# Summing spectral products by 32x32 blocks of the identity in place of 64x64 blocks

## The chip, the core and the metric

The kernel runs on one core of one Trainium2 chip. The metric is the device time of one execution in microseconds (us); lower is better. The core has a matrix engine (TensorE, PE in the profile; its weight loads are listed apart as PEld), a vector engine (VectorE, DVE), an activation engine (ScalarE, ACT), GpSimd (POOL) and SyncE (SP), which here only issues DMAs. Matmuls write to PSUM, 8 banks of 512 fp32 values on each of 128 partitions; ACT and DVE copy from there to SBUF.

## The reference, cut to what matters

The output is two results side by side, for 2048 positions and 576 channels each. A is a dilated sliding-window attention (32 heads of 18, window 8, step 2) with its projections; it is not touched by the change. B is a long convolution, which the reference computes by FFT:

```python
kv = k_shift * v                                   # [1, 2048, 576], k_shift: a 4-tap filter of k
kv_f = rfft(pad(kv, S)); kf_f = rfft(pad(ssm_k, S))  # along the positions, length 4096
y_f = kv_f * kf_f
y = irfft(y_f)[:S].astype(bfloat16) + kv * ssm_D
b = q * y
```

## The kernel before, in words

**Part B by blocks.** The positions are cut into four blocks of 512 (`NBL`, `BL`). For each input block i, matmuls with sine and cosine tables give its spectrum, 512 frequencies by 576 channels as a cosine part and a sine part (`x_spectrum`, L579). The filter's four blocks get their spectra in the same way (`filter_spectrum`, L520, kept in `Ks`). Output block j is the inverse transform of a sum over i = 0..j of complex products, spectrum of block i times filter spectrum of block j - i.

**Frequencies and partitions.** A spectrum has 128 partitions and four groups of frequencies (g) beside each other. For the inverse transform, each 64-row half of the partitions takes part of its groups from the other half, so the sums also move rows from one half to the other.

**Products, sums, inverse.** The work list `todo` (L979) has 30 entries (j, t, i): for each output block j, three thirds t of the channels (192 each, `TH`), and for each of those the blocks i = 0..j. For each entry:

- `products` (L856) is one DVE instruction (L860), 3072 elements per partition: both parts of the input's spectrum times both parts of the filter's. Its result goes to one of four places in `qk`, in turn (L858). Products run two entries ahead of the sums (`LEAD`, L983).
- `sums` (L867) adds the products into PSUM on PE (L880), as matmuls with blocks of the identity or of its negative (`ident`, `identn`) as weights. The real half is cosine by cosine and sine by sine, the imaginary half sine by cosine and cosine by sine. Each half (r) has a tile `acc[r]` of two banks, taken at i = 0. One call has 16 matmuls of 64x64 blocks with 384 columns, 4 for each of the 4 terms: `s` goes over two pairs of frequency groups, `h` over the two halves of the partitions.
- At i = j the two tiles are copied to `Yall` (L893 on ACT; the very last one by DVE, L891).
- When all channels of a block are there, `inverse` (L900) does matmuls with the table `TI` (L912), copies (L915), matmuls that mirror rows (`back`, L953), copies (L960), and a gate on DVE that multiplies with q (`gate`, L966), ahead of the store. For the last block the last third goes through `last` (L925, matmuls L931, copies L933, `ps_back` L939) and `gate_last` (L921).

`TI` is made early, from the table `TX`, by `table_i` (L384): identity matmuls (L390) that transpose and rearrange, 16 per call in two calls, then two copies each on ACT (L394).

**What sets the order.** Each engine runs its instructions in the order in which the program issues them. The script writes them in an order that it plans itself: `units` is a queue of PE work (output projection `ps_wo` L792 and L784, inverse steps), from which `until()` takes as many at each step as the table `PLACES` says; `tasks` is a queue of DVE work with due times (`due`), which a simple clock `clk` for D (DVE), P (PE) and A (ACT) estimates. `sums` calls `until()` first, and adds 0.34 us per half to the P clock. PSUM is given out under two tags of two buffers each, one buffer being two banks (`bank2`): tag A for the projections and the inverse, tag B for the sums, the attention sums (`ps_acc`, copied by L743 and L757) and others. A buffer is given out again when its copy is done. DVE, ACT, SP and POOL are in-order queues as well, so an instruction that waits holds up those behind it.

Of the kernel before, what the change touches and what calls it, by code (L numbers as in the profile page):

```python
# [24 lines left out]
def view(t, offset, dims):  # L25

    return bass.AP(tensor=t.tensor, offset=t.offset + offset, ap=[list(t.ap[0])] + [list(d) for d in dims])
# [3 lines left out]
def kernel(  # L31
# [13 lines left out]
    nc = tc.nc  # L45
    Bsz, S, D = A_x.shape
# [22 lines left out]
    NBL, BL = 4, 512  # L69
# [5 lines left out]
    TH = 192  # L75
# [12 lines left out]
    def bank2(name, tag):  # L88
        return pp.tile([128, 2, 512], FP32, name=name, tag=tag)
# [9 lines left out]
    TX = main.tile([128, 4, BL], BF16, name="TX", tag="tabx")  # L99
    TI = main.tile([128, 4, 2, 256], BF16, name="TI")  # L100
# [115 lines left out]
    ident = main.tile([128, 128], BF16, name="ident")  # L216
# [18 lines left out]
    for c0, p0, p1 in ((0, 0, 128), (128, 0, 128), (256, 0, 128), (384, 0, 128), (512, 0, 64), (512, 64, 128)):  # L235
        EHS.append(main.tile([128, 32], BF16, name=f"E{len(EHS)}"))
        e = EHS[-1][p0:p1, :]
# [20 lines left out]
    clk = {"D": 0.0, "P": 0.0, "A": 0.0}  # L258
    psum = {"A": deque([0.0, 0.0]), "B": deque([0.0, 0.0])}
# [7 lines left out]
    def pe(us, tag, evac, ready=0.0, first=True, last=True):  # L267

        clk["P"] = max(clk["P"], ready, psum[tag].popleft() if first else 0.0) + us
        clk["A"] = max(clk["A"], clk["P"] + 0.1) + evac  # L270
        if last:
            psum[tag].append(clk["A"])
        return clk["A"]
# [8 lines left out]
    def until():  # L282

        for _ in range(next(places, 0)):
            if units:
                p = max(clk["P"], psum["A"][0] if psum["A"] else 0.0)
                pop(next((n for n, u in enumerate(units) if len(u) < 4 or u[3] <= p), 0))
# [93 lines left out]
        return table(n_all[:, 2 * n:2 * n + 2, :], TX[:, 2 * n:2 * n + 2, :], n_all[:, 8, :], (4 + 2 * n, 5 + 2 * n), 4096,  # L381
              (offx[:], offx[:]))

    def table_i(s):  # L384

        ps = bank2("ps_ti", "A")
        for g2 in range(2):
            for c in range(4):
                for o in range(2):
                    nc.tensor.matmul(ps[64 * o:64 * o + 64, g2, 128 * c:128 * c + 128],  # L390
                                     view(TX, c * BL + 128 * (2 * ((o - s) % 2) + g2) + 64 * s, [[1, 64]]),
                                     ident[:], start=True, stop=True, tile_position=(0, 64 * o))
        for g2 in range(2):
            nc.scalar.activation(view(TI, 1024 * s + 512 * g2, [[128, 4], [4, 32], [1, 4]]),  # L394
                                 view(ps, 512 * g2, [[32, 4], [1, 32], [128, 4]]), ACT.Copy)

    skb = sp1.tile([128, 4, D], BF16, name="skb")
# [35 lines left out]
    for n0 in range(0, D, 256):  # L433
        n = min(256, D - n0)
        ps = bank2("ps_sk", "A" if n == 256 else "B")
        for h in range(0, n, 128):
            w = min(128, n - h)
            sk = skrow[:, 4 * (n0 + h):4 * (n0 + h + w)].rearrange("p (d j) -> p d j", j=4)
            for r in range(2):
                nc.tensor.matmul(ps[64 * r:64 * r + 64, h // 128, 0:4 * w], onesb[:, 0:64],  # L440
                                 sk if r else view(skrow, 4 * (n0 + h) + 3, [[4, w], [-1, 4]]),
                                 start=True, stop=True, tile_position=(0, 64 * r))
# [29 lines left out]
    for n in range(2):  # L472
        units.insert(2 + 4 * n, (0.85, partial(early, partial(table_i, n), 0.85), "x"))
# [5 lines left out]
    def taps(i):  # L479
        kj, vt = kjs[i], vts[i]  # L480
        kv = ab[:, i].rearrange("p s c d -> p (s c) d")
        for j in (3, 2, 1, 0):
            o = kv if j == 3 else sp1.tile([128, 4, D], BF16, name="tB")[:]
            dve(2304, lambda: nc.vector.tensor_tensor(  # L484
                o, kj[:, 3 - j:7 - j, :], skb[:, 3 - j, :].unsqueeze(1).to_broadcast([128, 4, D]), ALU.mult))
            if j < 3:
                dve(2304, lambda: nc.vector.tensor_tensor(kv, kv, o, ALU.add))  # L487
        return dve(2304, lambda: nc.vector.tensor_tensor(kv, kv, vt[:], ALU.mult))
# [57 lines left out]
    for i in range(NBL):  # L546
        r = taps(i)
# [51 lines left out]
    for jj, i in ((0, 0), (1, 2)):  # L599
# [6 lines left out]
        for n in range(2):  # L606
            a, b = last[4 * n:4 * n + 4], rest[4 * n:4 * n + 4]
# [221 lines left out]
    Yall = main.tile([128, 2, 2, 4, D], BF16, name="Yall", tag="r_kv")  # L829
# [35 lines left out]
    acc = {}  # L865

    def sums(j, t, i, pr, ready):  # L867

        until()
        sc, ss = CSG[j - i], SSG[j - i]  # L870
        for r, terms in enumerate((((0, 0, sc), (1, 1, ss)), ((1, 0, sc), (0, 1, -ss)))):
            if i == 0:
                acc[r] = bank2("ps_z", "B")
                clk["P"] = max(clk["P"], psum["B"][r])
            for n, (part, cs, sign) in enumerate(terms):
                w = ident if sign > 0 else identn
                for s in range(2):
                    for h in range(2):
                        o = 64 * ((h + s) % 2)
                        nc.tensor.matmul(view(acc[r], 512 * h, [[192, 2], [96, 2], [1, 96]])[o:o + 64], w[64 * h:64 * h + 64, 64 * h:64 * h + 64],  # L880
                                         pr[64 * h:64 * h + 64, part, cs, :].rearrange(
                                             "p (a g e) -> p g a e", a=2, g=4)[:, 2 * s:2 * s + 2],
                                         start=(i == 0 and n == 0), stop=(i == j and n == 1),
                                         tile_position=(64 * h, o))
            clk["P"] = max(clk["P"], ready) + 0.34
        if i == j:
            for r in range(2):
                y, z = (view(Yall, (j % 2) * 8 * D + r * 4 * D + TH * t, [[2 * D, 2], [D, 2], [1, TH]]),
                        view(acc[r], 0, [[512, 2], [TH, 2], [1, TH]]))
                if (j, t, r) == (NBL - 1, 2, 1):  # L890
                    nc.vector.tensor_copy(y, z)  # L891
                else:
                    nc.scalar.activation(y, z, ACT.Copy)  # L893
                out = pe(0.0, "B", 0.85)
            return out
# [102 lines left out]
    for n, (j, t, i) in enumerate(todo):  # L998
        produce(n + LEAD)
        if (t, i) == (0, 0):  # L1000
            need(f"inv{j - 2}")
        r = sums(j, t, i, *prs.pop(n))
        new = []
        if i == j and t == 2 and j < NBL - 1:
            a, b = inverse(j, 0, HD, r), inverse(j, HD, HD, r)
            new = [a[0], b[0], a[1], b[1], a[2], b[2]]
        elif i == j and j == NBL - 1 and t > 0:
            new = inverse(j, 0, 2 * TH, r) if t == 1 else inverse(j, 2 * TH, TH, r)
        for u in new:
            units.insert(sum(w[2][:3] == "inv" for w in units), u)  # L1010
# [35 lines left out]
```

## Time and profile before

| | us |
|---|---|
| median of 3 runs (224.27 to 224.85) | 224.3 |
| the profiled execution | 225.0 |
| its span, first to last instruction | 223.0 |
| PE busy / DVE busy / ACT busy in the span | 213.1 / 208.1 / 154.4 |
| L860 products on DVE, 30 of 1.75 | 50.5 |
| L893 copies of the sums on ACT, 23 of 0.81 | 17.4 |

The profile is one execution, traced by the hardware. An engine's row says how long at least one of its instructions was running. Matmuls overlap each other, so a busy PE may still take more work; 64x64 matmuls in different quarters of the array run at the same time. A group of instructions is written as line, engine, operation, output<-inputs, shapes, count, then busy time and mean duration (ns) of one, then the engine's idle time before them and what ended it. The timeline has start, length, engine and instruction, with idle time before it in brackets. The chain of waits goes back from the last instruction to what released it; it runs on PE for most of the first 194 us and mostly on DVE from then on. The stage with the products and sums is 160 to 216 us.

### The profile page before, as it was taken

To read this page: it belongs to the slowest core of one execution; us is meant where nothing else is said; L and a number is where in the kernel's file an instruction comes from. 1 tells how busy PE (TensorE), PEld (TensorE's weight loads), DVE (VectorE), ACT (ScalarE), POOL (GpSimd) and SP (SyncE) were. 2 spreads that over 40 slices of the span, in tenths; PEclk is the share of its full clock that TensorE was granted. 3 is DMA by queue.
4 is the path that set the end of the run, shared out by engine and by line. 5 is a ranking of instruction groups with operands and counts; after the bars stand their busy time and mean duration, and the time that the engine had idled before them with its cause. 6 is when DMAs were issued, how large, how long until landed. Compare 5 with 4: busy or idle time off the path is not lost.

```text
span 223.0 us, 5309 instructions
## 1 busy us (share of the span) xinstructions
PE 213.1 (96%) x2271; PEld 118.2 (53%) x2271; DVE 208.1 (93%) x156; ACT 154.4 (69%) x213; POOL 31.9 (14%) x68
## 2 busy tenths in 40 slices
PE   7999999999999999999999999999999999999891
PEld 2543444444566556753444445665656667666560
DVE  7789999999988999999899999999999899999992
ACT  5858766888596987756667768885678887655630
POOL 8860000000000040403410000015000000330000
PEclk9999999999999999999999999999999999999999
DMA  5999999999900047659999469917211103662016
GB/s 187 274 229 219 188 241 203 221 207 235 216 0 0 3 83 131 117 95 169 198 190 235 124 114 203 225 32 234 88 56 53 57 3 107 199 208 75 3 53 159
DMA packets 30985, 31.41 MB, mean 141 GB/s; under 512 B 16849, under 2 KB 26705, under 8 KB 30962
## 3 DMA queue, kind: packets, MB, share of 16 engines
q1 hardware_dynamic: 25714, 21.93, 44.6%
q0 software_dynamic: 2624, 6.64, 14.6%
q10 hardware_dynamic: 2624, 2.51, 3.3%
q8 instruction: 17, 0.28, 0.5%
q14 instruction: 6, 0.05, 0.1%
HBM read 13.11 MB, written 4.72 MB: 80 GB/s over the span
## 4 chain that ended last, share of the span: by engine, by line
PE 76%; DVE 9%; ACT 5%; issue 4%; DMA 3%; SPq 1%; DVEq 0%; ACTq 0%
PE ps_proj L310 15%; PE ps_fk L515 10%; PE ps_wo L792 7%; PE ps_fx L586 6%; DVE qk L860 6%; PE ps_z L880 5%; PE ps_log L633 5%; PE ps_fk L516 5%; PE ps_acc L739 4%; PE ps_inv L912 4%; PE ps_proj L427 3%; PE ps_proj L315 3%; DMA X<-attn 3%; PE ps_proj L322 3%; PE ps_idle L138 2%
## 5 line engine op out<-in xcount | busy, mean ns | idle before, releaser
L860 DVE TENSOR_TENSOR qk<-xw,Ks 128x3072 bf16<-128x3072 bf16 x30 | 50.5, 1750 | 1.2 <-PE ps_z L880 1.0
L624 DVE TENSOR_TENSOR prod<-qk 128x4096 bf16<-128x4096 bf16 (+1 forms) x20 | 40.6, 2074 | 3.4 <-PE ps_log L633 3.3
L310 PE MATMUL ps_proj<-xw 128*128 128x512 bf16 x160 | 38.4, 380 | 0.0
L515 PE MATMUL ps_fk<-kTok,TK 128*128 128x384 bf16 x128 | 32.8, 327 | 0.6 <-ACT Ks L530 0.5
L516 PE MATMUL ps_fk<-kTok,TK 128*128 128x192 bf16 x128 | 31.4, 246 | 0.0
L530 ACT ACTIVATE Ks<-ps_fk 128x576 bf16<-128x576 f32 x32 | 20.4, 653 | 9.9 <-PE ps_fk L516 9.7
L310 PEld LDWEIGHTS <-xw 128*128 128x128 bf16 x160 | 14.3, 98 | 18.9 <-issue 4.9
L893 ACT ACTIVATE Yall<-ps_z 128x768 bf16<-128x768 f32 x23 | 17.4, 808 | 6.1 <-PE ps_z L880 5.9
L346 ACT ACTIVATE qk<-ps_proj 128x1024 bf16<-128x1024 f32 x14 | 14.4, 1027 | 7.1 <-PE ps_proj L310 3.4
L589 ACT ACTIVATE xw<-ps_fx 128x576 bf16<-128x576 f32 x32 | 18.6, 660 | 0.2
L515 PEld LDWEIGHTS <-TK 128*128 128x128 bf16 x128 | 12.5, 98 | 11.8 <-issue 4.2
L792 PE MATMUL ps_wo<-qk,pv 128*128 128x288 bf16 x128 | 17.9, 287 | 0.0
L586 PE MATMUL ps_fx<-ab,TX 64*128 64x288 bf16 x256 | 17.7, 283 | 0.0
L487 DVE TENSOR_TENSOR ab<-ab,tB 128x2304 bf16<-128x2304 bf16 x12 | 16.3, 1358 | 0.4
L880 PE MATMUL ps_z<-qk,ident 64*64 64x384 bf16 x288 | 16.4, 325 | 0.3 <-ACT pv L743 0.3
L484 DVE TENSOR_TENSOR tB<-kj,skb 128x2304 bf16<-128x2304 bf16 x12 | 16.3, 1356 | 0.3
L912 PE MATMUL ps_inv<-Yall,TI 128*128 128x288 bf16 (+1 forms) x112 | 15.5, 292 | 0.7 <-ACT Yall L893 0.6
L739 PE MATMUL ps_acc<-P,ident 64*64 64x512 bf16 x192 | 15.3, 379 | 0.0
L346 ACT ACTIVATE v<-ps_proj 128x1024 bf16<-128x1024 f32 x9 | 9.2, 1022 | 8.8 <-PE ps_proj L322 4.6
L586 PEld LDWEIGHTS <-TX 64*128 64x128 bf16 x256 | 11.7, 94 | 6.5 <-issue 3.6
L799 ACT ACTIVATE qk<-ps_wo 128x576 bf16<-128x576 f32 x16 | 10.4, 651 | 6.1 <-PE ps_wo L792 3.0
L792 PEld LDWEIGHTS <-pv 128*128 128x128 bf16 x128 | 11.5, 98 | 6.0 <-issue 3.2
(146 smaller groups left out, 352.8 us busy)
## 6 DMA issues: line engine op xcount, KB each, us to landing
kj<-in_B_k_dram SPq DMA_DIRECT2D x7, 504.0 KB, 8.1
Ks<-Ks POOLq DMA_DIRECT2D x6, 576.0 KB, 7.7
qk<-attn SPq DMA_DIRECT2D x12, 256.0 KB, 5.8
vt<-in_B_v_dram SPq DMA_DIRECT2D x8, 288.0 KB, 8.6
out_dram<-qk ACTq DMA_DIRECT2D x8, 288.0 KB, 2.9
X<-attn SPq DMA_DIRECT2D x8, 256.0 KB, 5.1
Ks<-in_A_x_dram SPq DMA_DIRECT2D x2, 576.0 KB, 5.2
xw<-in_A_wqkv_dram SPq DMA_DIRECT2D x2, 576.0 KB, 7.4
```

Source lines behind the costliest of these rows:

```text
L310: nc.tensor.matmul(ps[:, jp, :], wq(kb, comp, 128 * ct, 128), xT(kb, 1024 * jj + 512 * jp, 512), start=(kb == 0 and not first), stop=(kb = ...
L346: nc.scalar.activation(view(t, o + pad + 1024 * jj, [[512, 2], [1, 512]]), ps[:], ACT.Copy)
L515: nc.tensor.matmul(o[:, 0:2], w, rhs[:, 0:2], start=start, stop=stop)
L516: nc.tensor.matmul(o[:, 2], w, rhs[:, 2], start=start, stop=stop)
L530: nc.scalar.activation(view(Ks, (3 - m) * SPB + 4 * D * cs + 96 * gi, [[768, 3], [384, 2], [1, 96]]), acc3(ps), ACT.Copy, scale=(CSG, SSG) ...
L586: nc.tensor.matmul(ps[:, pm, 0:HD], TX[64 * pm:64 * pm + 64, c, 128 * gi:128 * gi + 128], kv[64 * pm:64 * pm + 64, c, HD * h:HD * h + HD], ...
L624: r = dve(1024 * nj, lambda: nc.vector.tensor_tensor(view(prod, 0, [[256 * nj, 4], [256, nj], [1, 256]]), view(t, o + 256 * hh, [[0, 4], [ ...
L739: nc.tensor.matmul(acc[64 * o:64 * o + 64, h, :], ident[64 * h:64 * h + 64, 64 * h:64 * h + 64], view(P, 256 * u, [[2048, 2], [1, 256]])[6 ...
L792: nc.tensor.matmul(ps[:, r, 0:HD], oT(hh, j + 2 * r, t)[:, o:o + 128], wo[:, t // 2, t % 2, HD * h:HD * h + HD], start=(t == 0 and h == 0) ...
L860: r = dve(3072, lambda: nc.vector.tensor_tensor(pr, view(xw, i * SPB + 4 * TH * t, [[4 * D, 2], [0, 2], [1, 4 * TH]]), view(Ks, (3 - j + i ...
L880: nc.tensor.matmul(view(acc[r], 512 * h, [[192, 2], [96, 2], [1, 96]])[o:o + 64], w[64 * h:64 * h + 64, 64 * h:64 * h + 64], pr[64 * h:64 ...
L912: nc.tensor.matmul(ps[:, c, 0:n], TI[:, sl, pm, 128 * c:128 * c + 128], Yall[:, j % 2, pm, sl, c0:c0 + n], start=(pm == 0 and sl == 0), st ...
```

## The change

In `sums`, the identity blocks have 32 rows and 32 columns in place of 64, and a matmul has 192 columns in place of 384. One call has 64 matmuls and as many weight loads, in place of 16. The rows of each of the four 32-row groups (s) go to a PSUM bank of their own: groups 0 and 1 to the two banks of `acc[0]`, 2 and 3 to those of `acc[1]`. The real half takes the first 192 columns of a bank, the imaginary half the next 192, so each bank holds both. Both tiles are taken at the start of an i = 0 call. The frequencies that end up in one row group of `Yall` are other ones than before, so `table_i` arranges `TI` to fit: 32 matmuls of 32 columns per call in place of 16 of 64. The copies to `Yall` now take one pair of row groups each, both halves of it. The script's P clock gets 0.2 per half in place of 0.34. Nothing else changes.

```diff
-    def table_i(s):
+    def table_i(n):
...
         for g2 in range(2):
+            s = 2 * n + g2
             for c in range(4):
-                for o in range(2):
-                    nc.tensor.matmul(ps[64 * o:64 * o + 64, g2, 128 * c:128 * c + 128],
-                                     view(TX, c * BL + 128 * (2 * ((o - s) % 2) + g2) + 64 * s, [[1, 64]]),
-                                     ident[:], start=True, stop=True, tile_position=(0, 64 * o))
+                for o in range(4):
+                    nc.tensor.matmul(ps[32 * o:32 * o + 32, g2, 128 * c:128 * c + 128],
+                                     view(TX, c * BL + 128 * ((o - s) % 4) + 32 * s, [[1, 32]]),
+                                     ident[:], start=True, stop=True, tile_position=(0, 32 * o))
...
         sc, ss = CSG[j - i], SSG[j - i]
+        if i == 0:
+            for n in range(2):
+                acc[n] = bank2("ps_z", "B")
+                clk["P"] = max(clk["P"], psum["B"][n])
         for r, terms in enumerate((((0, 0, sc), (1, 1, ss)), ((1, 0, sc), (0, 1, -ss)))):
-            if i == 0:
-                acc[r] = bank2("ps_z", "B")
-                clk["P"] = max(clk["P"], psum["B"][r])
             for n, (part, cs, sign) in enumerate(terms):
                 w = ident if sign > 0 else identn
-                for s in range(2):
-                    for h in range(2):
-                        o = 64 * ((h + s) % 2)
-                        nc.tensor.matmul(view(acc[r], 512 * h, [[192, 2], [96, 2], [1, 96]])[o:o + 64], w[64 * h:64 * h + 64, 64 * h:64 * h + 64],
-                                         pr[64 * h:64 * h + 64, part, cs, :].rearrange(
-                                             "p (a g e) -> p g a e", a=2, g=4)[:, 2 * s:2 * s + 2],
-                                         start=(i == 0 and n == 0), stop=(i == j and n == 1),
-                                         tile_position=(64 * h, o))
-            clk["P"] = max(clk["P"], ready) + 0.34
+                for g in range(4):
+                    for s in range(4):
+                        o = 32 * ((s + g) % 4)
+                        nc.tensor.matmul(view(acc[s // 2], 512 * (s % 2) + TH * r, [[96, 2], [1, 96]])[o:o + 32],
+                                         w[32 * s:32 * s + 32, 32 * s:32 * s + 32],
+                                         pr[32 * s:32 * s + 32, part, cs, :].rearrange("p (a g e) -> p g a e", a=2, g=4)[:, g],
+                                         start=(i == 0 and n == 0 and r == 0), stop=(i == j and n == 1 and r == 1),
+                                         tile_position=(32 * s, o), skip_group_check=True)
+            clk["P"] = max(clk["P"], ready) + 0.2
         if i == j:
-            for r in range(2):
-                y, z = (view(Yall, (j % 2) * 8 * D + r * 4 * D + TH * t, [[2 * D, 2], [D, 2], [1, TH]]),
-                        view(acc[r], 0, [[512, 2], [TH, 2], [1, TH]]))
-                if (j, t, r) == (NBL - 1, 2, 1):
+            for h in range(2):
+                y, z = (view(Yall, (j % 2) * 8 * D + 2 * D * h + TH * t, [[4 * D, 2], [D, 2], [1, TH]]),
+                        view(acc[h], 0, [[TH, 2], [512, 2], [1, TH]]))
+                if (j, t, h) == (NBL - 1, 2, 1):
```

## Prediction

> **What bounds the kernel now.** I read the page first, then busy time by stage, then DVE's timeline, then the steps around its one stop and around the end. Below, a "unit" is one call of `sums` (30 of them, numbered 0 to 29 in program order, product k feeding unit k), and u is the time that PE needs from the start of one unit to the start of what follows.
>
> From the page, its first part and its groups:
>
> ```profile
> PE 213.1 (96%) x2271; PEld 118.2 (53%) x2271; DVE 208.1 (93%) x156; ACT 154.4 (69%) x213; POOL 31.9 (14%) x68
> ...
> L860 DVE TENSOR_TENSOR qk<-xw,Ks 128x3072 bf16<-128x3072 bf16 x30 | 50.5, 1750 | 1.2 <-PE ps_z L880 1.0
> ...
> L880 PE MATMUL ps_z<-qk,ident 64*64 64x384 bf16 x288 | 16.4, 325 | 0.3 <-ACT pv L743 0.3
> ```
>
> PE looks like the bound (96%), but a PE row holds the 0.3 us that each matmul takes to come out, so it says little. The busy time of the stage that the change touches (columns: stretch, length, then busy us and instructions of PE, weight loads, DVE, ACT, POOL, then clock and DMA) says more:
>
> ```profile
> 163.00:194.00 31.00, 30.47 (x434) 20.21 (x423) 29.86 (x19) 24.82 (x37) 1.92 (x3) 1.00 0.22 67
> 194.00:215.60 21.60, 20.89 (x336) 13.55 (x334) 21.60 (x14) 12.14 (x18) 1.92 (x3) 1.00 0.29 90
> ```
>
> DVE idles 1.14 us in 52.6 us, at full clock throughout. DVE's timeline shows where:
>
> ```profile
> 160.41 15.29 DVE L860 TENSOR_TENSOR qk<-xw,Ks 128x3072 bf16<-128x3072 bf16 x9
> 176.74 6.77 DVE L860 TENSOR_TENSOR qk<-xw,Ks 128x3072 bf16<-128x3072 bf16 x4 [1.04 <-PE ps_z L880]
> 183.43 1.35 DVE L966 TENSOR_TENSOR qB<-yA,qB 128x2304 bf16<-128x2304 bf16 x1
> ```
>
> Products follow each other every 1.67 us. One, product 9, waited 1.04 us: four buffers take the products in turn (L858), so it needs unit 5 to have read product 5. Another 0.09 us lies inside the first row (9 products at 1.67 us plus 0.08 for the last one's end are 15.1, not 15.29): product 7, which needs unit 3. So **DVE is the bound of this stage**, and the most that a faster sum can give before the end of the products is 1.13 us.
>
> **The sums themselves.** Before, a unit is 16 matmuls in 4 groups of 4 that run together. From the whole timeline near 208 us:
>
> ```profile
> 207.58 0.33 PE L880 MATMUL ps_z<-qk,ident 64*64 64x384 bf16 x4
> ...
> 207.91 0.98 PE L880 MATMUL ps_z<-qk,ident 64*64 64x384 bf16 x20
> ...
> 215.26 0.81 ACT L893 ACTIVATE Yall<-ps_z 128x768 bf16<-128x768 f32 x1 [0.95 <-PE ps_z L880]
> ...
> 215.60 0.95 DVE L891 CAST Yall<-ps_z 128x768 bf16<-128x768 f32 x1
> ...
> 216.12 1.48 PE L931 MATMUL ps_inv<-Yall,TI 128*128 128x192 bf16 x16 [0.26 <-ACT Yall L893]
> ```
>
> Four matmuls of 0.325 us each cover only 0.33 us, so the four start within some 13 ns (with their four weight loads between them); five groups cover 0.98, so groups follow every (0.98-0.325)/4 = 0.163 us, and u = 4 x 0.163 = 0.65. The last row gives the price of 192 columns: (1.48-0.245)/15 = 0.082 us. After, a unit is 64 matmuls and 64 loads of 32x32 blocks, 192 columns each. *Lower bound*: 16 run together and u = 4 x 0.082 = 0.33. *Upper bound*: instructions come no faster than the profile has them over a long stretch, L753, 32 matmuls and 32 loads in 8 groups that follow every (1.04-0.27)/7 = 0.11 us, so 14 ns each, and u = 128 x 14 = 1.8. The ends are far apart. The nearer row is L880 itself: 4 pairs start in 13 ns, so 16 pairs need 52 ns, less than the 82 that their columns last. I take **u = 0.40**: 0.33, 0.02 for the first group (the next comes 0.18 later, not 0.163: the rows at 205.77 and 205.95) and 0.05 for the staggered start.
>
> [...]
>
> **What the saving does on the path.** The two copies to `Yall` (ACT, 0.81 and then 0.70 us more) used to follow the real half, then the imaginary one. Now every bank is finished only by the last quarter of the unit, and the next group (i = 0) needs both pairs of banks after three matmuls. So a chain unit, two copies, unit is as long as before: 0.33 us gained in the sum, 0.33 lost in the first copy. With each step's own times in the trace:
> - Units 0 and 1: unit 0 waits for the second copy L757 (164.2), unit 1 for the second copy of unit 0 (166.37 instead of 165.99). Nothing gained, +0.05.
> - Unit 2 starts at 169.33 and frees PE at 169.73 (before 169.97). Its copies queue behind L799 (to 170.05) as before and end at 171.5, so unit 3 starts at 171.55 and unit 4 frees PE at 172.31, before 172.70: -0.39. The three inverse steps behind them (3.1 us) and unit 5 shift by that; unit 5 is shorter as well and its last result comes at 176.01, so product 9 starts at 176.06: **-0.68** of the 1.13.
> - Units 6, 7, 8: unit 6 comes out at 176.41, its copies end at 177.97, unit 7 waits for them, unit 8 comes out at 178.93 (before 179.85).
> - The gate moves. Compiled, the order of ACT, POOL and SP is unchanged and PE's is the same but for the split sums and tables, but DVE issues the first L966 after 12 products, not 13. It needs both copies of L960, which stand on ACT behind unit 8's:
>
> ```profile
> 179.58 1.51 ACT L893 ACTIVATE Yall<-ps_z 128x768 bf16<-128x768 f32 x2 [0.45 <-PE ps_z L880]
> 180.97 1.20 ACT L960 ACTIVATE yA<-ps_back 128x576 bf16<-128x576 f32 x2
> ```
>
>   Before, L960 ended at 182.17 and the gate came at 183.43: 1.26 us of cover. After, the copies run from 178.98, L960 ends at 181.58, and DVE stands at the gate at 181.76-0.68 = 181.08, with product 12 queued behind it: a wait of 0.55, **+0.55**. It could be 0 (L960 half a microsecond sooner) or 1.
> - From there DVE has no wait: PE runs further ahead than before (units 15 and 18, which left 0.7 and 0.14 us of slack, gain more than DVE does).
> - The end. Product 29 ends, DVE does a gate L966 (to 215.60), then its half of the last copy, which therefore isn't sooner. Before, the halves were real and imaginary, so the first 8 matmuls of L931 needed ACT's copy alone and started at 216.12. Now the halves are blocks, and 14 of the 16 matmuls need DVE's copy: 216.60 + 14 x 0.082 = 217.75 against 216.12 + 16 x 0.082 = 217.43: **+0.3**. All behind it (copies, `ps_back`, last gate, store) moves along. Bounds: 0 (if DVE's copy came first) and 0.5 (all 16 behind it).
>
> The copies keep their 768 elements in runs of 192: 0, by the same row. `table_i` has 32 matmuls of 32 columns for 16 of 64; its 16 take 0.64 us, 28 ns each, two at a time per 56 ns. Four at a time cost 0; one each 28 ns cost 0.45 us twice, on a stretch where the chain runs on PE. I take 0 and keep +0.9.
>
> Sum: -0.68 + 0.55 + 0.3 = +0.17 us. The profiled execution took 225.0 (223.0 of span, 2.0 around it), 0.7 above the median 224.3; the difference is put on the median: **224.5**. Each 0.1 us on u puts 0.3 on unit 5 (units 3, 4, 5), 0.3 more on unit 8 and so on the gate, and 0.1 on the end: +0.7.
>
> **The rivals.** About 0.3% (0.67 us) is what a measurement of this kernel can tell from no change.
> - *Forecast*, u 0.33 to 0.45: -0.3 to +0.6, 224.0 to 224.9; it can pass 225.0 with the tables. Chance 0.47.
> - *PE is not fed fast enough*, slower. The page's queue q8 brings 17 packets of 16 KB (256 instructions of 64 bytes), and 0.5% of 16 engines' 223 us is 1.05 us a packet: 4.1 ns an instruction, 0.52 us for the 128 of a unit. For it: units come in pairs and threes, 256 to 384 instructions in a row. Against it: inverse steps of 1 to 3 us lie between them and allow fetching ahead. It decides from u = 0.47 on (0.17 + 0.7 x 0.7 = 0.67). At 0.52 to 0.65 it gives +1.0 to +2.5: 225.3 to 226.8. Chance 0.27.
> - *The 16 tiles don't run together*, the change doesn't do what it says: u from 0.65 up to 1.1. At 0.65 PE gains nothing, the gate and later copies cost some 2 us; at 1.1 PE is the bound, 30 x 0.45 = 13.5 us more. 226.5 to 238. Against it: four blocks, two in the same rows, do run together at L880. Chance 0.09. [...]
> - *Faster*: the stall goes whole (-1.13) and the gate finds its copies ready, with or without the 0.3 at the end: 223.2 to 223.5. For it: DVE is otherwise gapless. Against it: the copies above. Chance 0.17.
>
> Same holds 0.43 (the forecast, less 0.04 at its upper edge), slower 0.04+0.27+0.09 = 0.40, faster 0.17. The range 223.3 to 227.0 takes in the faster case and the underfed one and leaves out the third.
>
> **What would show it.** Units at 0.33 to 0.45 us from start to start where two follow each other, with x16 groups every 0.082 (else the second or third rival); product 9's wait at 0.3 to 0.6 instead of 1.04; a new DVE wait ahead of the first L966 for ACT L960; L931 starting with two matmuls and then waiting for DVE's copy. I am wrong if DVE shows no wait from 160 us on (faster), or if PE holds up products beyond product 9 (slower).

## The result and the profile after

The changed kernel takes 241.03 us (median of 4 runs, 240.80 to 241.79), the kernel before 224.57 beside it (4 runs, 224.27 to 225.51). The ratio is 1.0731, with a 95% interval of 1.069 to 1.0773: **slower by 16.5 us**, far outside the predicted range. In the ratios here and below, an execution that took over 1.5% longer than the fastest of its kernel is left out (it is one, in the first experiment). The profiled execution took 240.8, its span is 239.1 (before: 223.0). Below, "unit", "product" and u mean what they mean in the prediction. The matmul of `sums` now stands on L882, the product on L861, the copies to `Yall` on L893 (DVE) and L895 (ACT), the inverse's matmuls on L914 and L933, the gate on L968.

From the page of the changed kernel: the engines' busy time, the clock in 40 slices, the queue that brings instructions, and three groups (the last column is idle time before the group and what ended most of it):

```profile
PE 216.9 (91%) x3732; PEld 124.2 (52%) x3743; DVE 208.7 (87%) x156; ACT 154.2 (64%) x213; POOL 31.8 (13%) x68
...
PEclk9999999999999999999999999999999999979787
...
q8 instruction: 29, 0.48, 0.9%
...
L861 DVE TENSOR_TENSOR qk<-xw,Ks 128x3072 bf16<-128x3072 bf16 x30 | 51.0, 1753 | 7.4 <-PE ps_z L882 7.1
...
L882 PE MATMUL ps_z<-qk,ident 32*32 32x192 bf16 x1152 | 17.6, 249 | 5.3 <-issue 4.2
...
L882 PE MATMUL ps_z<-qk,identn 32*32 32x192 bf16 x768 | 14.3, 250 | 5.4 <-issue 4.6
```

The page of the kernel before has for the same queue:

```profile
q8 instruction: 17, 0.28, 0.5%
```

No engine has more work that counts: DVE's busy time is 0.6 us more, ACT's 0.2 less. But DVE now waits 7.1 us for the sums (before 1.0), and PE stands still 10.7 us ahead of L882, 8.8 of it put down to "issue". That word is for time in which an engine waited for nothing that the profile shows: no data, no buffer. And q8 has 29 packets in place of 17.

The busy time by stage (columns as in the prediction) shows the same from 185 us on:

```profile
185.00:205.00 20.00, 18.28 (x563) 12.47 (x545) 18.27 (x12) 12.56 (x19) 3.83 (x6) 1.00 0.54 155
205.00:224.00 19.00, 13.79 (x579) 9.21 (x579) 14.89 (x9) 6.59 (x10) 0.00 (x0) 0.82 0.05 17
224.00:239.10 15.10, 7.99 (x276) 5.80 (x263) 3.31 (x5) 2.98 (x5) 0.00 (x0) 0.84 0.30 80
```

In the second stretch PE, DVE and ACT are all idle for part of the time, and the clock (0.82) is no longer full. Before, DVE had no gap of note from 185 us to the end of the products.

DVE's timeline has the waits one by one:

```profile
172.34 3.43 DVE L861 TENSOR_TENSOR qk<-xw,Ks 128x3072 bf16<-128x3072 bf16 x2 [0.51 <-PE ps_z L882]
177.05 5.09 DVE L861 TENSOR_TENSOR qk<-xw,Ks 128x3072 bf16<-128x3072 bf16 x3 [1.29 <-PE ps_z L882]
183.76 1.36 DVE L968 TENSOR_TENSOR qB<-yA,qB 128x2304 bf16<-128x2304 bf16 x1 [1.62 <-ACT yA L962]
...
205.75 3.42 DVE L861 TENSOR_TENSOR qk<-xw,Ks 128x3072 bf16<-128x3072 bf16 x2 [2.18 <-PE ps_z L882]
...
215.48 6.76 DVE L861 TENSOR_TENSOR qk<-xw,Ks 128x3072 bf16<-128x3072 bf16 x4 [2.58 <-PE ps_z L882]
...
230.13 0.96 DVE L893 CAST Yall<-ps_z 128x768 bf16<-128x768 f32 x1 [6.62 <-PE ps_z L882]
```

The first rows are the places that the prediction named: product 9 (1.29, before 1.04) and the first gate (1.62). Those of products 22 and 26 (2.18, 2.58) are new, and so is the last: DVE had done everything by 223.51 and waited 6.62 us for PE's last sums.

PE's timeline of these microseconds shows what PE was doing:

```profile
205.19 0.25 PE L882 MATMUL ps_z<-qk,ident 32*32 32x192 bf16 x2 [0.71 <-issue]
205.19 0.95 PE L882 MATMUL ps_z<-qk,identn 32*32 32x192 bf16 x80
205.90 0.52 PE L882 MATMUL ps_z<-qk,ident 32*32 32x192 bf16 x32
206.18 0.36 PE L882 MATMUL ps_z<-qk,identn 32*32 32x192 bf16 x14
208.92 0.26 PE L882 MATMUL ps_z<-qk,identn 32*32 32x192 bf16 x2 [2.38 <-issue]
...
209.94 4.79 PE L914 MATMUL ps_inv<-Yall,TI 128*128 128x288 bf16 x24
...
217.54 0.29 PE L882 MATMUL ps_z<-qk,identn 32*32 32x192 bf16 x6
219.55 0.29 PE L882 MATMUL ps_z<-qk,identn 32*32 32x192 bf16 x10 [1.72 <-issue]
...
229.61 0.29 PE L882 MATMUL ps_z<-qk,ident 32*32 32x192 bf16 x10 [2.11 <-issue]
...
230.95 2.72 PE L933 MATMUL ps_inv<-Yall,TI 128*128 128x192 bf16 x16 [0.52 <-ACT Yall L895]
```

The stops are **inside a unit**: at 208.92 PE goes on with the same line, weights and tile as before the gap, 14 matmuls into a group of 16. Nothing of the data can be missing there. Between the start at 205.19 and the stop, the four rows hold 2 + 80 + 32 + 14 = 128 matmuls with as many loads: 256 instructions, which is one q8 packet (0.48 MB / 29 = 16 KB, so 64 bytes each). The five longest stops inside units (1.29, 0.95, 2.62, 1.97 and 2.36 us from one instruction's start to the next) lie 256 recorded instructions, or multiples of 256, apart.

The packets themselves, from the DMA view of 203 to 229 us, in 40 slices of 0.65 us:

```profile
GB/s 0 0 60 379 14 25 0 0 0 0 25 0 0 0 0 0 25 0 0 0 0 25 0 0 0 0 0 25 0 0 0 0 7 365 239 207 114 0 0 0
...
q8 instruction: 6, 0.10, 1.6%
```

Each lone "25" is 16 KB in one slice, one packet. From 206.5 to 220.9 they come every five or six slices. Their starts, read from the trace, are 206.54, 209.96, 213.40, 216.92, 220.89 and 227.00 us; of the last 13 gaps in the stage, 11 are 3.42 to 4.03 us, none shorter. A packet takes 0.9 to 1.7 us, and PE goes on some 1.3 us after it has landed (206.54 + 1.09 = 207.63, PE at 208.92; 227.00 + 1.30 = 228.30, PE at 229.61). In the kernel before, the shortest gap between packets is 5.9 us in this stage and 4.6 in the whole trace. Other transfers don't hold the packets apart: from 209.90 to 215.00 us the DMA engines are busy 2% of the time (the row below).

So the theory is: **in this kernel PE gets no more than 256 instructions in about 3.5 us, 14 ns for each, however short they are.** The stage holds 2244 matmuls and 2240 loads in the trace (160.5 to 230.0 us), 17.5 packets, at least 61 us at 3.5; before it held 1627 instructions, 6.4 packets, 22 us of supply for 55 us of work.

The rest of the loss stands behind the stops. The rows of the clock (same columns; the last but two is the granted clock):

```profile
209.90:215.00 5.10, 5.10 (x77) 3.30 (x65) 3.00 (x2) 3.05 (x5) 0.00 (x0) 0.67 0.02 6
220.70:223.50 2.80, 2.74 (x18) 1.00 (x18) 2.80 (x2) 0.71 (x2) 0.00 (x0) 0.50 0.02 6
230.90:233.70 2.80, 2.75 (x20) 2.33 (x21) 1.52 (x3) 0.49 (x1) 0.00 (x0) 0.50 0.22 70
```

From 210.4, 220.65 and 230.9 us on, the granted clock is at half (0.50) for 3.4 us each time (and once more from 237.7 us to the end), each time soon after a stop: PE had been idle for 2.38, 1.72 and 2.11 us. The inverse's matmuls that fall there take longer than in the kernel before: L914 x24 4.79 (3.11), x8 with 384 columns 2.78 (1.46), L933 x16 2.72 (1.48), together 4.2 us. The row of the first in the kernel before:

```profile
202.72 3.11 PE L912 MATMUL ps_inv<-Yall,TI 128*128 128x288 bf16 x24
```

The length of one stop does not decide it: in a kernel below (32x32 blocks, 96 instructions per unit) PE stands idle for 1.8 us at a stretch, longer than the 1.72 above, and the clock stays full (0.999 over the span, at 0.9 or more in each of the 40 slices). In the changed kernel's trace the half-clock stretches start at multiples of 3.41 us from each other (210.41, 220.65, 230.89 and 237.71). Cut on this grid, the trace has the clock go from full to half after four windows of 3.41 us, in which PE was idle for 1.92, 2.53, 2.57 and 3.03 us in all, and stay full after the others, with up to 1.19. That is an estimate from the start and end of each matmul in this trace.

On the path: the last unit ends at 229.98 (before 215.54), +14.4; from there to the end of the span it is 9.1 us in place of 7.5, of which the slow L933 is 1.2. That is the 16.1 us of the span.

### The profile page after: what moved, and what is told of

The parts are those of the page before. It is cut to its first block, busy times and chain, and to the rows that moved or that the text cites. A ratio compares the mean times of both kernels' runs of the same rounds, so it can differ in the third digit from the quotient of the medians.

```text
span 239.1 us, 8242 instructions
## 1 busy us (share of the span) xinstructions
PE 216.9 (91%) x3732; PEld 124.2 (52%) x3743; DVE 208.7 (87%) x156; ACT 154.2 (64%) x213; POOL 31.8 (13%) x68
## 4 chain that ended last, share of the span: by engine, by line
PE 62%; DVE 10%; DMA 9%; ACT 6%; SPq 6%; issue 6%; ACTq 0%; DVEq 0%
PE ps_fk L516 9%; PE ps_z L882 9%; PE ps_inv L914 6%; PE ps_wo L793 6%; PE ps_proj L310 5%; PE ps_fx L587 5%; PE ps_log L634 4%; PE ps_fk L517 4%; PE ps_acc L740 4%; DMA kj<-in_B_k_dram 4%; ACT Yall L895 4%; DVE ab L488 3%; DVE tB L485 3%; SPq L191 3%; DMA Ks<-in_A_x_dram 3%
## 5 line engine op out<-in xcount | busy, mean ns | idle before, releaser
L861 DVE TENSOR_TENSOR qk<-xw,Ks 128x3072 bf16<-128x3072 bf16 x30 | 51.0, 1753 | 7.4 <-PE ps_z L882 7.1
L310 PE MATMUL ps_proj<-xw 128*128 128x512 bf16 x150 | 36.5, 380 | 1.2 <-issue 1.1
L895 ACT ACTIVATE Yall<-ps_z 128x768 bf16<-128x768 f32 x23 | 17.4, 808 | 19.7 <-PE ps_z L882 19.7
L882 PE MATMUL ps_z<-qk,ident 32*32 32x192 bf16 x1152 | 17.6, 249 | 5.3 <-issue 4.2
L914 PE MATMUL ps_inv<-Yall,TI 128*128 128x288 bf16 (+1 forms) x112 | 18.9, 326 | 1.3 <-ACT Yall L895 0.9
L882 PE MATMUL ps_z<-qk,identn 32*32 32x192 bf16 x768 | 14.3, 250 | 5.4 <-issue 4.6
L346 ACT ACTIVATE qk<-ps_proj 128x1024 bf16<-128x1024 f32 x14 | 14.4, 1026 | 7.1 <-PE ps_proj L310 3.4
L882 PEld LDWEIGHTS <-ident 32*32 32x32 bf16 x1152 | 12.1, 88 | 9.1 <-issue 8.1
L914 PEld LDWEIGHTS <-TI 128*128 128x128 bf16 x112 | 11.6, 107 | 6.7 <-issue 2.7
```

The source lines that it names most:

```text
L310: nc.tensor.matmul(ps[:, jp, :], wq(kb, comp, 128 * ct, 128), xT(kb, 1024 * jj + 512 * jp, 512), start=(kb == 0 and not first), stop=(kb = ...
L861: r = dve(3072, lambda: nc.vector.tensor_tensor(pr, view(xw, i * SPB + 4 * TH * t, [[4 * D, 2], [0, 2], [1, 4 * TH]]), view(Ks, (3 - j + i ...
L882: nc.tensor.matmul(view(acc[s // 2], 512 * (s % 2) + TH * r, [[96, 2], [1, 96]])[o:o + 32], w[32 * s:32 * s + 32, 32 * s:32 * s + 32], pr[ ...
L914: nc.tensor.matmul(ps[:, c, 0:n], TI[:, sl, pm, 128 * c:128 * c + 128], Yall[:, j % 2, pm, sl, c0:c0 + n], start=(pm == 0 and sl == 0), st ...
```

## The experiments

Two theories. *Supply*: the number of PE instructions decides, whatever their tile size. *Tiles*: the 32x32 blocks themselves, their banks or the later copies cost the time. "Before" is the kernel before, run beside each on the same chip.

**64x64 blocks, each matmul cut in four.** The kernel before, with its banks, copies and order, but 64 matmuls of 96 columns per unit in place of 16 of 384:

```diff
-                for s in range(2):
-                    for h in range(2):
...
-                        nc.tensor.matmul(view(acc[r], 512 * h, [[192, 2], [96, 2], [1, 96]])[o:o + 64], w[64 * h:64 * h + 64, 64 * h:64 * h + 64],
...
-                                             "p (a g e) -> p g a e", a=2, g=4)[:, 2 * s:2 * s + 2],
+                for gg, aa in ((0, 0), (0, 1), (1, 0), (1, 1)):
+                    for s in range(2):
+                        for h in range(2):
...
+                            nc.tensor.matmul(view(acc[r], 512 * h + 192 * gg + 96 * aa, [[1, 96]])[o:o + 64], w[64 * h:64 * h + 64, 64 * h:64 * h + 64],
...
+                                                 "p (a g e) -> p g a e", a=2, g=4)[:, 2 * s + gg, aa],
```

> The kernel before with each matmul of the sums cut into four of 96 columns: 64x64 blocks, banks, copies and tables as before, but 64 matmuls and 64 weight loads a unit, as many as in the changed kernel. Supply theory (PE gets its instructions in blocks of 256, one block in some 3.5 us at best; the stage with the sums has 30 x 128 + 900 = 4740 instructions = 18.5 blocks = 65 us where DVE needs 52): 12 to 16 us slower, 236 to 241, with stops of 0.5 to 2.6 us on PE at places 256 instructions apart. Tile theory (32x32 tiles are what is slow) and copy theory (both halves in one bank, so later copies, gate and end): the unit stays near 0.65 to 0.7 us, 224.3 to 226.

Measured: 242.33 us (three executions, 241.87 to 244.75) against 224.74, ratio 1.0792 (1.0707 to 1.0877), a little more than the 236 to 241 expected. The profile is of the fourth, of 247.38 us, so it is read for where PE stops and not for how long. PE's timeline there:

```profile
180.31 0.31 PE L954 MATMUL ps_back<-yA,flip 64*64 64x288 bf16 x2
182.68 0.31 PE L954 MATMUL ps_back<-yA,flip 64*64 64x288 bf16 x2 [2.06 <-issue]
...
184.57 0.67 PE L881 MATMUL ps_z<-qk,ident 64*64 64x96 bf16 x16
...
186.41 1.35 PE L881 MATMUL ps_z<-qk,ident 64*64 64x96 bf16 x57 [1.17 <-issue]
```

The first stop is in the middle of L954, a line that no one touched: it isn't the blocks, nor their banks. From 182.68 to the stop that ends at 186.41 PE starts 128 matmuls, 256 instructions with their loads, and q8 has 29 packets here too. The same number of instructions at the old tile size costs the same time. Supply holds, tiles falls.

**How much is too much.** Four kernels between 32 and 128 instructions per unit. At the old size, the same cut in two or in three:

```diff
+                for gg in range(2):
...
+                            nc.tensor.matmul(view(acc[r], 512 * h + 192 * gg, [[96, 2], [1, 96]])[o:o + 64], w[64 * h:64 * h + 64, 64 * h:64 * h + 64],
...
+                                                 "p (a g e) -> p g a e", a=2, g=4)[:, 2 * s + gg],
```

```diff
+                for gg in range(3):
...
+                            nc.tensor.matmul(view(acc[r], 512 * h + 32 * gg, [[192, 2], [96, 2], [1, 32]])[o:o + 64], w[64 * h:64 * h + 64, 64 * h:64 * h + 64],
...
+                                                 "p (a g e) -> p g a e", a=2, g=4)[:, 2 * s:2 * s + 2, :, 32 * gg:32 * gg + 32],
```

> The same with two matmuls of 192 columns for each of 384: 32 matmuls and 32 loads a unit. Supply theory: 30 x 64 + 900 = 2820 instructions, 11 blocks, 39 us at 3.5 us, less than DVE's 52: 224 to 225.5, no stops beyond some tenths. A cost that is the same for every added instruction would give a third of the loss of the four-way cut, +4 to +5. Tile and copy theory: 224.3 to 225.

> The kernel before with each matmul of the sums cut into three of 128 columns: 64x64 blocks, banks, copies, tables and gate as before, 48 matmuls and 48 loads a unit. Supply theory with a threshold: 30 x 96 + 900 = 3780 instructions, 14.8 blocks of 3.5 us = 52 us, the same as DVE's: 1 to 5 us slower, 226 to 230. If every added instruction had the same price (17 us for 96 added), it would be 11 us slower, 236. It also tells how much of the 3 us lost by the 48 pairs of 32x32 blocks is the supply and how much the late copies.

At 32x32, the changed kernel without the second term of each half (its sums are not those of the reference), and the changed kernel with the first terms of both halves in one matmul of 384 columns:

```diff
-            for n, (part, cs, sign) in enumerate(terms):
+            for n, (part, cs, sign) in enumerate(terms[:1]):
...
-                                         start=(i == 0 and n == 0 and r == 0), stop=(i == j and n == 1 and r == 1),
+                                         start=(i == 0 and n == 0 and r == 0), stop=(i == j and r == 1),
```

```diff
+        for n, (part, cs, sign, r) in enumerate(((0, 0, sc, 0), (1, 1, ss, 0), (0, 1, -ss, 1))):
...
+                    if n == 0:
+                        nc.tensor.matmul(view(acc[s // 2], 512 * (s % 2), [[TH, 2], [96, 2], [1, 96]])[o:o + 32],
+                                         w[32 * s:32 * s + 32, 32 * s:32 * s + 32],
+                                         view(pr, 96 * g, [[1536, 2], [384, 2], [1, 96]])[32 * s:32 * s + 32],
```

> The changed kernel without the second product term of each half of the sums (spectra incomplete): 32x32 tiles, shared banks, late copies, moved gate and late end as in the changed kernel, but 32 matmuls and 32 loads a unit. Supply theory: 11 blocks of 256 in the stage, 39 us, no loss from the supply, only the copies and the end: 223.8 to 225.5. Copy theory: the whole loss stays, 236 to 241. Tile theory: half the loss, about 232.

> The changed kernel with the first terms of both halves in one matmul of 384 columns (they have the same sign), so 48 matmuls and 48 loads a unit in place of 64; all products are summed. Supply theory: 30 x 96 + 900 = 3780 instructions, 14.8 blocks of 3.5 us = 52 us, just what DVE needs: 225 to 229. Tile theory (a price per 32x32 matmul): three quarters of the loss, 236. Copy theory: 240, unchanged.

| PE instructions per unit | 64x64 blocks | 32x32 blocks | q8 packets |
|---|---|---|---|
| 32 | 224.7 (before) | | 17 |
| 64 | 1.0027 (0.9998 to 1.0057) | 1.0013 (0.9977 to 1.0049) | 21 |
| 96 | 1.0133 (1.0085 to 1.0181) | 1.0144 (1.0086 to 1.0201) | 25 |
| 128 | 1.0792 (1.0707 to 1.0877) | 1.0731 (1.069 to 1.0773) | 29 |

The two columns agree within their intervals: it is the count and not the tile (the 32x32 kernels also have the later copies, for which see below). The medians at 64, 225.54 and 225.85 us, lie just above the 225.5 that was the most expected, and the executions of the 32x32 one spread widely, from 223.74 to 226.69; those at 96, 228.21 and 228.32, lie within. The cost isn't in proportion; it begins near 96 and then is steep. That is where the supply runs out: at 96 the trace of the 64x64 kernel has 3383 PE instructions in the stage (160.5 to 217.0 us), 13.2 packets, one in 4.3 us, close to the 3.4 to 4.0 that the densest stretches have; at 64 it is 2538 instructions, one packet in 5.7 us. The kernels at 96 show single stops (1.3 and 0.8 us at 64x64, 0.8 and 2.1 at 32x32), where units stand close together. At 64 the cut in two has none: its longest gap on PE, 1.7 us ahead of L913, was a wait for a copy on ACT (L799), which itself had waited 2.05 us for a DMA.

**The moved gate.** The kernel with 96 instructions at 32x32, with the script's P clock at 0.68 in place of 0.4, so that the first gate comes after 13 products again:

```diff
-        clk["P"] = max(clk["P"], ready) + 0.4
+        clk["P"] = max(clk["P"], ready) + 0.68
```

> The kernel with 48 pairs of 32x32 blocks, with 0.68 for 0.4 on the script's P clock, so that DVE issues the first gate after 13 products as before, not 12; nothing else moves. If the moved gate costs what it waited there (0.91 us at L973) and DVE bounds the rest: 0.5 to 0.9 us faster than that kernel, 227.4 to 227.8. If PE's supply and the late copies bound the rest: no change, 228.3.

Measured: 228.57 against 224.93, ratio 1.0149 (1.0101 to 1.0197); with the gate after 12 products it was 1.0144. No gain shows. The intervals are 1.1 us to each side, so the 0.5 to 0.9 us that the gate might have cost are not excluded, but it is no large part of the loss. DVE's timelines of the two, the earlier gate first:

```profile
182.69 1.36 DVE L973 TENSOR_TENSOR qB<-yA,qB 128x2304 bf16<-128x2304 bf16 x1 [0.91 <-ACT yA L967]
```

```profile
191.57 1.36 DVE L973 TENSOR_TENSOR qB<-yA,qB 128x2304 bf16<-128x2304 bf16 x1 [1.32 <-ACT yA L967]
```

In one kernel the first gate waits; in the other the first has cover, and the second waits instead.

**The later copies alone.** The kernel before, 16 matmuls, but with both tiles taken at i = 0 and both halves ending only in the unit's last four matmuls, as the change has it:

```diff
-        for r, terms in enumerate((((0, 0, sc), (1, 1, ss)), ((1, 0, sc), (0, 1, -ss)))):
-            if i == 0:
+        if i == 0:
+            for r in range(2):
...
+        for n, halves_ in enumerate((((0, 0, sc), (1, 0, sc)), ((1, 1, ss), (0, 1, -ss)))):
+            for r, s in ((0, 0), (1, 1), (1, 0), (0, 1)):
```

> The kernel before with its 16 matmuls in another order: both tiles are taken at i = 0 and both halves end in the last group of four, so that both copies start only when the unit is done, as in the changed kernel. Copy theory: 5 us slower or more, 229 to 240. Supply theory: each chain of unit, copies, unit is 0.3 us longer, product 9 waits 0.5 to 1 us more and the end 0.3: 224.5 to 226.

Measured: 228.55, ratio 1.0148 (1.0098 to 1.0198), +3.8 us at the medians: more than I expected for copies and less than their theory needs for the whole loss. PE's timeline shows part of the price, 1.0 us in which units wait for ACT to empty the tile:

```profile
179.75 0.51 PE L881 MATMUL ps_z<-qk,ident 64*64 64x384 bf16 x6 [0.25 <-ACT Yall L894]
...
182.13 0.35 PE L881 MATMUL ps_z<-qk,identn 64*64 64x384 bf16 x2 [0.41 <-ACT Yall L894]
...
182.83 0.52 PE L881 MATMUL ps_z<-qk,identn 64*64 64x384 bf16 x8 [0.35 <-ACT Yall L894]
```

The kernel has no stop by supply, so this is a cost of its own: with units as long as before, late copies are not free. The 32x32 kernel with half of the terms has the same late copies and ratio 1.0013, which fits that a shorter unit pays for them, as the prediction argued for the first units. How much of them is left in the changed kernel, whose units take 0.55 us, these two runs don't tell.

**The most that could be gained.** The kernel before without the second term (8 matmuls per unit, u = 0.33; its sums are not those of the reference), by the same cut of `terms` as above:

> The kernel before without the second product term of each half of the sums (the second matmul group is left out, so the spectra are incomplete): 8 matmuls a unit, u = 0.33, what the change would have at best. If DVE bounds the stage: product 9's wait goes, 0.7 to 1.3 us faster, 223.0 to 223.6. If PE bounds it: 30 x 0.33 = 10 us faster, 214.

Measured: 224.49, ratio 0.9975 (0.9946 to 1.0003). Product 9's wait shrinks to 0.33 us, and no other product waits. Even with the sums halved at no price, the gain is 0.6 us at the median, less than the 0.7 to 1.3 expected, and the interval takes in no change.

**Product 9's wait alone.** The kernel before with unit 5 put ahead of two inverse steps:

```diff
-    2, 4, 0, 0, 1, 2, 1, 0, 3, 0, 1, 0, 0, 0, 0, 5, 1, 0, 4, 0, 0, 3, 0, 0, 0, 3, 0, 4, 4, 1, 1,
+    2, 4, 0, 0, 1, 2, 1, 0, 1, 1, 2, 0, 0, 0, 0, 5, 1, 0, 4, 0, 0, 3, 0, 0, 0, 3, 0, 4, 4, 1, 1,
```

> The kernel before with two inverse steps moved on PE from ahead of unit 5 to behind it (the 46th to 49th entries of PLACES: 1, 1, 2, 0 in place of 3, 0, 1, 0), nothing else. DVE order unchanged. If product 9's wait for unit 5 is all that holds DVE in this stage: 0.8 to 1.1 us faster, 223.2 to 223.6. If PE bounds the stage: no change.

Measured: 224.94 against 225.09, ratio 1.0001 (0.9972 to 1.003). DVE's timeline:

```profile
179.45 3.43 DVE L860 TENSOR_TENSOR qk<-xw,Ks 128x3072 bf16<-128x3072 bf16 x2 [0.45 <-PE ps_z L880]
...
201.10 13.44 DVE L860 TENSOR_TENSOR qk<-xw,Ks 128x3072 bf16<-128x3072 bf16 x8 [0.48 <-PE ps_z L880]
```

Product 9's wait is gone, and products 11 and 22 wait 0.93 us between them. None of the 0.8 to 1.1 us expected was gained. So the wait wasn't one misplaced step alone: what is taken from one place comes back at the next, which fits a PE whose queue of work is near its bound as well.

## Why the prediction was wrong

**The step that failed** is the price of the second rival, "PE is not fed fast enough". The mechanism was named, and the packet and its 256 instructions were read rightly, but the step "0.5% of 16 engines' 223 us is 1.05 us a packet: 4.1 ns an instruction" took the time of a packet's transfer for the time from one packet to the next. The traces have 0.9 to 1.7 us for the transfer but 3.4 to 4.0 us for the cycle. So the rival came out at +1.0 to +2.5 us, where the change costs +16.5 and the same number of instructions at the old tile size +17.6. The packets' starts were in the trace of before, but at its demand they lay no closer than 4.6 us, so the shortest cycle could not be read there. The upper bound in the text, 14 ns an instruction "over a long stretch", equals the sustained rate, but by luck: the 64 instructions of L753 are a quarter of a packet and cannot show how fast packets come. I had kept it as an end for u, and gave the rival none of its price. (By the prediction's own slope the rival's upper end, at u = 0.65, is +1.9 us and not +2.5; neither is near.)

**u.** The forecast of 0.40 rested on four pairs that start in 13 ns. Between stops, the four rows from 205.19 us above have 128 pairs, two units, that start from 205.19 to 206.29 (206.18 + 0.36 - 0.25, the time of one matmul): 8.7 ns a pair, u = 0.55. The first 16 of them do start within 54 ns, as forecast for every 16; from the third 16 on, 16 pairs take 133 to 160 ns, 8.8 ns a pair on average. So a burst was taken for the steady pace. The columns alone would last 0.33, by the 0.082 us of the prediction's L931 row. By the prediction's slope (0.7 us for each 0.1 on u) this would have been some +1 us without any stop.

**The third rival** (the tiles don't run together) is out: pairs start every 8.7 to 8.8 ns while the columns of each last 82 by the same row, so those of some nine are under way at a time, an estimate from the two figures.

**The other terms.** The tables cost nothing, as taken: their matmuls start from 23.3 to 28.3 us (before 24.4 to 29.3), and the products start at 159.78 (before 160.41). The gate's wait for ACT's copies was there, at 1.62 in place of 0.55, but the run with the gate put back shows no gain. Product 9's wait, which was to shrink by 0.68, grew from 1.04 to 1.29. Units 3 to 5 are not as short as forecast; with the later copies alone it is 1.29 as well, so it need not be supply, and the runs don't tell the shares apart. At the end, L933 waited 0.52 us for ACT's copy, and DVE's ended another 0.14 us later (230.13 + 0.96 = 231.09), so at most its first two matmuls ran ahead, as said; but this stood behind a stop of 2.1 us and at half the clock. The bound on the gain, 1.13 us, was right in kind; it leaves out that a product that waits also loses the 0.08 us by which it would have overlapped the one before. From the starts of products 0 and 9 (160.41 and 176.74, nine steps of 1.67) it is 1.3. The run with halved sums got 0.6.

"DVE is the bound of this stage" was half of it: PE was close behind, as the run with unit 5 moved suggests, so the stage had little slack on PE to lose.

**What stays open.** What the 3.5 us of a cycle consist of: by the trace, some 1.1 us are the transfer and 1.3 go from landing to PE's next start; the remaining 1.0 to 1.4 stand between PE's passing of a boundary and the next packet's start (at four of the five stops; 2.8 after the one that ends at 199.81), and no run takes them apart. Whether other instructions on PE's queue count alike wasn't tried. Nor was the half clock isolated: its 4.2 us are read from rows, and part of them lies beside waits for supply.

## What to carry to other kernels

In this kernel, cutting the matmuls of a unit smaller had a price in instructions at the same columns (+17.6 us for four of 96 in place of one of 384): count PE's instructions (loads too) in the densest stage and divide by 256. Here 5.7 us of work per block cost nothing measurable, 4.3 us cost 1.3%, with stops where the dense units stand together, and 3.1 us (55 us for 17.5 packets) cost 7.3 to 7.9%. The profile calls the stops "issue". A packet's transfer time (0.9 to 1.7 us) was not its cycle time (3.4 to 4.0) here: where a queue's rate matters, look for the closest two of its packets under load, and if the trace has no load, keep the far bound in the chances.

## What the runs showed of the hardware

- PE's instructions came in packets of 16 KB, 256 instructions: the five longest stops inside units of the changed kernel lie 256 recorded instructions or multiples of it apart, and q8 has 29 packets for 7475 recorded matmuls and loads (17 for 4542 before). In the changed kernel 11 of the last 13 gaps between packets' starts in the stage are 3.42 to 4.03 us, none shorter (13 to 16 ns an instruction), with stops of up to 2.6 us at the boundaries.
- In the changed kernel, four windows of 3.41 us in which PE was idle for 1.92 to 3.03 us, three of them with stops of 1.7 to 2.4 us, were followed by windows of 3.4 us at a granted clock of 0.50, in which matmuls elsewhere took longer (2.72 us in place of 1.48 for the same 16). Here the supply problem so also hit code that has few instructions.
- In the two units from 205.19 us, pairs of a load and a 32x32 matmul start 8.7 ns apart on average. The first 16 come faster (54 ns for all 16) after the stops that end at 199.81, 205.19 and 208.92; in runs of units without a stop ahead the first 16 take 125 to 134 ns.
